# Tap sums and the turn of the filter gradient moved from the matmul stream to DMA and VectorE in the last phase

## The chip, the cores and the metric

The kernel runs on one core of a Trainium2 chip. The metric is the device time of one execution in microseconds (us), the median of several. Five engines work side by side, each through its own queue in order: TensorE (matmuls and weight loads), VectorE (in the profile DVE), ScalarE (ACT), GpSimd (POOL) and SyncE (SP), which here issues most of the DMA transfers. A DMA queue entry named SPq is the issue of a transfer by SyncE, not the movement of its bytes.

## The reference

With S = 2048 rows (time), D = 1024 channels and F = 3584:

```python
xn = layernorm(q)
k_shift = sum over t of shift(k, t) * shift_k[:, 3 - t]        # 4 taps, causal
kv = k_shift * v
y = causal_conv(kv, ssm_k) + kv * ssm_D                        # one filter of length S per channel
h = relu(xn @ W_gate) * (xn @ W_up)
out = q + xn * y + h @ W_down
```

It returns `out` and the gradients for q, k, v, shift_k, ssm_k, ssm_D, W_gate, W_up and W_down, given the gradient g of `out`, in bf16. Two of them matter here. With gks the gradient of k_shift, the gradient of shift_k is, for each channel c and tap i, the sum over time of gks[t, c] * k[t - i, c]: 4 numbers per channel. The gradient of ssm_k is gh[c, t], a row of 2048 per channel (channel-major), while the kernel's other tensors are time-major, [t, c].

## The kernel before

Two bodies of work share the core. `LnMlp` does the layer norm and the gated MLP with its gradients, nearly all large matmuls (128x128 weights, 512 columns), in phases: `hidden`, `grad_down`, `grad_in`, `out_phase`, `grad_x`. `ABranch` does the convolution by way of Fourier transforms, themselves small matmuls, for eight groups of 128 channels. Its steps are generators (`slots`, `wide_slots`): each `yield p, d` names a piece of TensorE work p and a piece of VectorE work d. The loop at the end of the kernel function interleaves the branch with the MLP's phases: every piece of MLP work takes its nanoseconds from a budget `left`, and while the budget is at or below zero the branch takes a step and gives back the price of its slot (`SLOT` 1900, or `DENSE` 1900 with TensorE work and 1250 without). The budget starts at `A_START`, so the branch starts that much later than the MLP. While the branch runs, each engine's instructions keep the order in which they are written. The branch ends before `grad_in` does; then `open_right` starts to load W_down for `out_phase`.

What the change touches, per group: `inv_b` is the last step of an inverse transform; it writes a tile time-major, with 64x32 weights and 512 columns (16 matmuls). `inv_b_chan` is the same step for the filter gradient, but with data as weights, 128x128 with 64 columns (32 matmuls), so that the result is channel-major (`ghn`), and `store_gh` writes it to `out_gh` in rows of 2 KB; it also copies element 0 of each row, the gradient of ssm_D, into `gD_all`. `tap_sums` multiplies, for each of 16 row blocks and each of 4 quarters of the channels, gks (128x32) with four shifted views of k (128 columns): 64 matmuls, of which only the diagonals are wanted. `tap_diagonals` takes them out on VectorE with an identity mask and a reduction into `gs_all`. At the end `small_outputs` turns the collected sums with six transposes on TensorE and stores them. `store_time` writes a time-major tile of 2048x128 to memory in two transfers with runs of 256 bytes.

`grad_x`, the last phase, goes over 16 tiles of 128 rows. For each it loads two tall tiles transposed by DMA (`ggT`, `guT`: 128 x 3584, turned, 28 blocks of 128x128; pool `hT` with three buffers), three row tiles (gt, gy, xn), runs 2 x 56 matmuls into two PSUM banks of four (`ps_x`), and VectorE evicts each with a sum and goes on to the layer norm's gradient:

```python
V.tensor_tensor_reduce(out=gx[:, oc], in0=ps, in1=gy[:, oc], scale=1.0, scalar=0.0, op0=ALU.add,
                       op1=ALU.add, accum_out=m[:, ob:ob + 1])
```

SyncE issues all of these transfers in one queue. In it stand, tile after tile, ggT of the next tile, gt, the two stores of the tile before, gy, xn, then guT.

Of the kernel before, what the change touches and what calls it, by code (L numbers as in the profile page):

```python
# [11 lines left out]
BF16 = mybir.dt.bfloat16  # L12
F32 = mybir.dt.float32
I32 = mybir.dt.int32
ALU = mybir.AluOpType
ACT = mybir.ActivationFunctionType
AX = mybir.AxisListType
P = 128
# [3 lines left out]
class Pri:  # L22
# [4 lines left out]
    def __init__(self, tc):  # L27
        self.tc = tc
        self.n = 0
        self.strict = False  # L30
# [15 lines left out]
NB1 = 32  # L46


class ABranch:
# [5 lines left out]
    def __init__(self, tc, pri, S, D, k, v, g, shift_k, ssm_k, ssm_D, xn_d, y_d, sk_d, out_gk, out_gv, out_gsk,  # L55
                 out_gh, out_gsD):
        assert S == 2048 and D % P == 0
        self.tc, self.nc, self.pri = tc, tc.nc, pri
        self.S, self.D, self.NG = S, D, D // P
        self.k, self.v, self.g, self.shift_k, self.ssm_k, self.ssm_D = k, v, g, shift_k, ssm_k, ssm_D  # L60
        self.xn_d, self.y_d, self.sk_d = xn_d, y_d, sk_d
        self.out_gk, self.out_gv, self.out_gsk, self.out_gh, self.out_gsD = out_gk, out_gv, out_gsk, out_gh, out_gsD
        self.pools, self.pin, self.dense, self.queue = [], False, False, []
        self.cap, self.turns = 2, 0
# [83 lines left out]
    def tables(self):  # L148
        nc, con, big, pri = self.nc, self.con, self.big, self.pri
        pri.late()  # L150
        V, hold = nc.vector, self.tc.keep_in_program_order
# [5 lines left out]
        self.gs_all = con.tile([P, self.NG, 4], F32, name="gs_all")  # L157
        self.gD_all = con.tile([64, 2, self.NG], BF16, name="gD_all")
# [77 lines left out]
        self.ident32 = con.tile([P, 1, 32], BF16, name="ident32")  # L236
        self.NX = con.tile([1, 3, P], BF16, name="NX")
        V.memset(self.NX[:], 0.0)
        for b in range(0, P, 32):
            V.tensor_copy(out=self.ident32[b:b + 32, 0, :], in_=self.identA[b:b + 32, b:b + 32])  # L240
# [81 lines left out]
    def load_taps(self, st):  # L322
        skb = st["skb"] = self.sm.tile([P, 4, 1, P], BF16, name="skb")
        self.load(skb[:].rearrange("p i o c -> p (i o c)"),
                  self.sk_d[4 * st["gi"]:4 * st["gi"] + 4, :].rearrange("i c -> (i c)").partition_broadcast(P))
# [174 lines left out]
    def inv_b_chan(self, st, half):  # L500
        dst, Cf = self.ttile("ghn"), self.flp[:, half]
        st["ghn"] = dst
        dv = dst[:, 0:16, :].rearrange("p r c -> p (r c)").rearrange("p (n1 n2) -> p n1 n2", n2=NB1)
        for n0 in range(0, NB1, 16):
            ps, at = self.banks("h n c", n=8)
            for n in range(16):
                self.mm(at(n // 8)[:, n % 8, :], Cf[:, n0 + n, :], self.RB[:].rearrange("p h n -> p (h n)"))
            self.evict(ps, "p h n c -> p c (h n)", lambda s: dv[:, :, n0 + 8 * s.start:n0 + 8 * s.stop])
        yield

    def store_gh(self, st):
        ghf = st["ghn"][:, 0:16, :].rearrange("p r c -> p (r c)")
        ghv = ghf.rearrange("p (h t) -> p h t", h=2)
        self.vcopy(self.gD_all[:, :, st["gi"]:st["gi"] + 1], ghv[0:64, :, 0:1])
        for b in range(2):
            self.store(self.out_gh[st["cg"], 1024 * b:1024 * b + 1024].rearrange("(h c) t -> c h t", h=2),
                       ghv[64 * b:64 * b + 64])
# [7 lines left out]

    def tap_sums(self, st):

        gks, kp = st["gks"], st["kp"]
        pd = self.banks("h x")[1](0)[:, 0:P].rearrange("p (i c) -> p i c", i=4)
        for r in range(16):  # L530
            for b in range(0, P, 32):
                self.mm(pd[b:b + 32], gks[:, r, b:b + 32], kp[:, r:r + 4, b:b + 32], start=(r == 0), stop=(r == 15))
        st["pd"] = pd

    def tap_diagonals(self, st):
        dg = self.tmp.tile([P, 4, 32], F32, name="dg", tag="tmp")
        self.tt(dg[:], st["pd"], self.ident32[:].to_broadcast([P, 4, 32]), ALU.mult)
        self.pri.late()
        self.pri.pin(self.nc.vector.tensor_reduce(out=self.gs_all[:, st["gi"], :], in_=dg[:], axis=AX.X, op=ALU.add))
# [33 lines left out]
    def steps(self):  # L573

        sk_t = self.shift_rows()
        self.pin = True
        yield 10000
        self.load(self.sk_d, sk_t[:])  # L580
        yield 25000
        self.sts = [dict(gi=gi, cg=slice(gi * P, (gi + 1) * P)) for gi in range(self.NG)]
        st = self.sts[0]
        self.load_filter(st)
        self.issue()
        yield 3400
        self.load_k(st)
        self.load_taps(st)
        yield 3400
        self.load_g(st)  # L590
        yield 3400
        self.load_v(st)
        yield 6800
        self.load_xn(st)
        self.pin = False
        self.pri.strict = True
        self.open_arena()
        self.begin(st)
        for st in self.sts:
            for p, d in (self.wide_slots if self.dense else self.slots)(st, st["gi"]):  # L600
                *more, last = self.parts(p)
                for fs in more:
                    self.all_of(fs)
                    yield self.DENSE[0]
                self.all_of(last)
                self.run(d)
                if self.queue and not self.hold():
                    self.issue()
                yield self.DENSE[p is None] if self.dense else self.SLOT
        self.small_outputs()  # L610
# [61 lines left out]
    def slots(self, st, gi):  # L672
# [57 lines left out]
        self.store_time(self.out_gv, st["cg"], gv)  # L730
        yield None, q
        yield None, self.both(lambda: self.halo(st), q)
        yield lambda: self.tap_sums(st), None
# [7 lines left out]
        yield None, lambda: self.tap_diagonals(st)  # L741
# [42 lines left out]
        yield self.inv_b_chan(st, 1), tk  # L784
        yield None, tk
        yield None, tk
        if last:
            yield None, lambda: self.store_gh(st)
            return
        self.need(self.load_v, nx)  # L790
        yield None, lambda: self.start_kvt(nx)
        f1k = self.fwd1(self.Bk, nx["kvt"])
        yield None, lambda: self.store_gh(st)
# [11 lines left out]
    def wide_slots(self, st, gi):  # L805
# [61 lines left out]
        self.store_time(self.out_gv, st["cg"], gv)  # L867
        yield None, q
        yield None, self.both(lambda: self.halo(st), q)
        yield lambda: self.tap_sums(st), None  # L870
# [7 lines left out]
        yield None, lambda: self.tap_diagonals(st)  # L878
# [43 lines left out]
        yield self.inv_b_chan(st, 1), tk  # L922
        yield None, tk
        yield None, None
        if last:
            yield None, lambda: self.store_gh(st)
            return
        self.need(self.load_v, nx)
        yield None, lambda: self.start_kvt(nx)
        f1k = self.fwd1(self.Bk, nx["kvt"])  # L930
        yield None, lambda: self.store_gh(st)
# [11 lines left out]
    def small_outputs(self):  # L943
        nc, NG = self.nc, self.NG
        tp = nc.tensor.transpose
        sk = self.sm.tile([P, NG, 4], BF16, name="sk_o", bufs=1)
        self.vcopy(sk[:], self.gs_all[:])
        ps = self.ps.tile([P, 1024], BF16, name="ps8", tag="aps")
        for i in range(4):
            self.pri.now()  # L950
            self.pri.pin(tp(ps[0:NG, i * P:(i + 1) * P], sk[:, :, 3 - i], self.identA[:]))
        for h in range(2):
            self.pri.now()
            self.pri.pin(tp(ps[0:NG, 4 * P + 64 * h:4 * P + 64 * h + 64], self.gD_all[:, h, :], self.identA[0:64, 0:64]))
        so = self.tmp.tile([NG, 5, P], BF16, name="so", tag="tmp")
        self.vcopy(so[:, 0:4, :].rearrange("g i c -> g (i c)").rearrange("g (c i) -> g i c", i=4),
                   ps[0:NG, 0:4 * P].rearrange("g (i c) -> g i c", i=4))
        self.vcopy(so[:, 4, :], ps[0:NG, 4 * P:5 * P])
        self.store(self.out_gsk.rearrange("(g c) i -> g (c i)", c=P), so[:, 0:4, :].rearrange("g i c -> g (i c)"))
        self.store(self.out_gsD.rearrange("(g c) -> g c", c=P), so[:, 4, :])  # L960
A_START = 60_000


class LnMlp:
# [742 lines left out]
    def grad_x(self, x, g, xn_d, y_d, h_d, ug_d, Wd, out0, out1):  # L1707
        nc, tc, D, V = self.nc, self.tc, self.D, self.nc.vector
        p_ev = tc.alloc_tile_pool(name="x_ev", bufs=2, side="right")
        p_sm = tc.alloc_tile_pool(name="x_sm", bufs=2, side="right")  # L1710
        for st in range(self.ST):
# [12 lines left out]
            if st == 1:  # L1724
                self.rest_load(x, xn_d, y_d, Wd)
            gx = p_ev.tile([P, D], F32, name="gx")
# [34 lines left out]
        self.p_rest.release()  # L1761
        p_sm.release()
# [8 lines left out]
def kernel(  # L1771
# [33 lines left out]

    sk_d = dram.tile([D // P * 4, P], BF16, name="sk_d")
# [3 lines left out]
    a = ABranch(tc, pri, S, D, A_k[0], A_v[0], g, A_shift_k, A_ssm_k, A_ssm_D, xn_d, y_d, sk_d[:], out_2[0], out_3[0],  # L1810
                out_4, out_5, out_6)
# [38 lines left out]
    b.grad_x(x, g, xn_d, y_d, h_d, ug_d, B_W_down, out_0[0], out_1[0])  # L1850
# [30 lines left out]
```

## Time and profile before

| | |
|---|---|
| time, median of 3 | 1876.04 us (1875.87 to 1876.24) |
| span of the profiled execution | 1874.5 us |
| TensorE busy | 1852.7 us, 99% |
| VectorE busy | 1050.2 us, 56% |
| ScalarE busy | 613.1 us, 33% |
| moved by DMA | 323.72 MB, mean 173 GB/s |
| the branch's matmuls | from 124.9 to 1244 us |
| `out_phase` begins | 1290.8 us |
| `grad_x` begins | 1478 us |

Busy time of an engine is the union of its instructions' spans. Matmuls overlap in the array, so TensorE's busy share says that it is occupied, not that it runs at its peak. A line of matmul groups gives weights, columns, count, busy time and mean duration of one; a window gives for each engine the busy time in that stretch, then the granted clock of TensorE, the mean busy share of the 16 DMA engines and the rate. That share can come out over 1, since records of packets overlap.

### The profile page before, as it was taken

The page shows a single profiled execution, that of the slowest core. Times are in us where ns is not written, and L with a number is a line of the kernel's source. Part 1 is how long each engine was busy: PE and PEld are TensorE (multiplying, and loading weights), DVE is VectorE, ACT ScalarE, POOL GpSimd, SP SyncE. Part 2 cuts the span into 40 slices and gives each one's busy share as a digit, 9 for nine tenths or more (in the row PEclk, how much of TensorE's full clock was granted, in tenths as well). Part 3 has the DMA queues.
Part 4 walks back from the last instruction along what each step waited for, and adds up shares of the span by engine and source line. Part 5 has one row for each costly group of instructions (what it writes and reads, how often), then busy time and mean ns, then how long its engine had stood idle before and what let it go on. Part 6 is the DMA issues. An engine that isn't in the chain of part 4 may idle for free.

```text
span 1874.5 us, 32572 instructions
## 1 busy us (share of the span) xinstructions
PE 1852.7 (99%) x13478; PEld 852.5 (45%) x13707; DVE 1050.2 (56%) x1537; ACT 613.1 (33%) x904; POOL 14.8 (1%) x37
## 2 busy tenths in 40 slices
PE   9999999999999999999999999999999999999999
PEld 4444444444444444444444444444444544444444
DVE  6656888699698677685585876710222222222222
ACT  5745444534445445444535454320000000000000
POOL 1000000000000000000000000000000000000000
PEclk9999999999999999999999999999999999999999
DMA  9897499868568747377465353479999945555553
GB/s 254 257 246 169 134 204 222 193 166 200 150 163 209 246 100 192 104 185 216 136 148 153 97 165 98 136 172 278 259 226 249 249 115 123 124 123 124 124 124 73
DMA packets 695509, 323.72 MB, mean 173 GB/s; under 512 B 524864, under 2 KB 664896, under 8 KB 695360
## 3 DMA queue, kind: packets, MB, share of 16 engines
q1 hardware_dynamic: 684864, 300.78, 65.1%
q10 hardware_dynamic: 9216, 16.65, 2.9%
q0 software_dynamic: 1280, 4.20, 0.6%
q8 instruction: 107, 1.75, 0.4%
q14 instruction: 42, 0.34, 0.1%
HBM read 143.79 MB, written 95.44 MB: 128 GB/s over the span
## 4 chain that ended last, share of the span: by engine, by line
PE 97%; issue 1%; DMA 1%; DVE 0%; SPq 0%; ACT 0%; POOL 0%; ACTq 0%; POOLq 0%
PE ps_x L1739 21%; PE ps_w L1503 20%; PE ps_u L1171 10%; PE ps_h L1171 10%; PE ps_o L1670 10%; PE ps_g L1171 10%; PE ps_d L1503 9%; PE ps L89 4%; PE ps_d L1518 1%; PE ps_c L89 1%; PE ps_w L1518 1%; PE ps_r L1700 0%; PE ps_warm L1226 0%; DMA wu<-in_B_W_up_dram 0%; SPq L1189 0%
## 5 line engine op out<-in xcount | busy, mean ns | idle before, releaser
L1503 PE MATMUL ps_w<-ugs,xn_nat 128*128 128x512 bf16 x1672 | 377.1, 380 | 4.5 <-issue 2.4
L1171 PEld LDWEIGHTS <-xnT 128*128 128x128 bf16 x1792 | 170.8, 98 | 208.9 <-issue 8.2
L93 ACT CAST arena<-ps 128x1024 bf16<-128x1024 f32 x240 | 234.3, 1021 | 72.2 <-PE ps L89 62.9
L1503 PEld LDWEIGHTS <-xn_nat 128*128 128x128 bf16 x1728 | 164.4, 98 | 201.3 <-issue 9.8
L344 DVE STREAM_TRANSPOSE arena<-arena 128x1024 f32<-128x1024 f32 x96 | 180.4, 1933 | 129.1 <-ACT arena L93 115.6
L1171 PE MATMUL ps_u<-wu,xnT 128*128 128x512 bf16 x875 | 205.3, 380 | 1.4 <-issue 0.3
L1171 PE MATMUL ps_g<-wg,xnT 128*128 128x512 bf16 x867 | 203.1, 380 | 2.4 <-issue 0.6
L1171 PE MATMUL ps_h<-wdT,goT 128*128 128x512 bf16 x862 | 202.8, 380 | 2.6 <-issue 0.8
L1757 ACT ACTIVATE w<-xn,m 128x512 f32<-128x512 bf16 x32 | 24.3, 806 | 553.0 <-issue 317.2
L1739 PE MATMUL ps_x<-wgT,ggT 128*128 128x512 bf16 x879 | 197.6, 379 | 0.9
L1739 PE MATMUL ps_x<-wuT,guT 128*128 128x512 bf16 x877 | 197.5, 379 | 1.0
L1670 PE MATMUL ps_o<-wd,hT 128*128 128x512 bf16 (+1 forms) x878 | 186.6, 373 | 0.9
L1503 PE MATMUL ps_d<-g_nat,hs 128*128 128x512 bf16 x740 | 168.8, 380 | 2.1 <-issue 0.8
L1739 PEld LDWEIGHTS <-guT 128*128 128x128 bf16 x896 | 87.7, 98 | 105.7
L1739 PEld LDWEIGHTS <-ggT 128*128 128x128 bf16 x896 | 87.7, 98 | 105.5
L1171 PEld LDWEIGHTS <-goT 128*128 128x128 bf16 x896 | 85.5, 98 | 105.4 <-issue 5.5
L1670 PEld LDWEIGHTS <-hT 128*128 128x128 bf16 x896 | 87.7, 98 | 100.0
L1506 ACT CAST wi<-ps_w 128x512 bf16<-128x512 f32 x108 | 63.8, 591 | 200.5 <-PE ps_w L1503 180.2
L1741 DVE CUSTOM_DVE_ANT_0 gx<-ps_x,gy 128x512 f32<-128x512 f32 x32 | 22.1, 692 | 185.3 <-PE ps_x L1739 175.4
L1413 ACT CAST gh<-ps_h 128x512 bf16<-128x512 f32 x112 | 65.5, 585 | 184.1 <-PE ps_h L1171 173.2
L1286 DVE SCALAR_TENSOR_TENSOR ru<-ru,ps_u 128x512 bf16<-128x512 bf16 x112 | 76.5, 684 | 81.9 <-PE ps_u L1171 44.4
L97 DVE TENSOR_TENSOR t<-arena 128x2048 bf16<-128x2048 bf16 x96 | 114.1, 1219 | 0.4
(165 smaller groups left out, 1341.6 us busy)
## 6 DMA issues: line engine op xcount, KB each, us to landing
ug_d<-ru SPq DMA_DIRECT2D x112, 256.0 KB
ugs<-ug_d SPq DMA_DIRECT2D x112, 256.0 KB
wg<-in_B_W_gate_dram SPq DMA_DIRECT2D x56, 256.0 KB
wu<-in_B_W_up_dram SPq DMA_DIRECT2D x56, 256.0 KB
h_d<-ht SPq DMA_DIRECT2D x112, 128.0 KB
hs<-h_d SPq DMA_DIRECT2D x56, 256.0 KB
out_dram<-wi SPq DMA_DIRECT2D x56, 256.0 KB
gt<-in_grad_out_dram SPq DMA_DIRECT2D x32, 256.0 KB
```

Source lines behind the costliest of these rows:

```text
L89: self.pri.pin(self.nc.tensor.matmul(out, lhsT=lhsT, rhs=rhs, start=start, stop=stop))
L93: self.pri.pin(self.nc.scalar.copy(out=out, in_=in_))
L97: self.pri.pin(self.nc.vector.tensor_tensor(out=out, in0=in0, in1=in1, op=op))
L344: self.pri.pin(self.nc.vector.transpose(out=df[:, c0:c0 + 32, :], in_=sf[:, c0:c0 + 32, :]))
L1171: self.pri.pin(self.nc.tensor.matmul(ps[:], lhsT=xT[:, kt * P:(kt + 1) * P], rhs=w(kt), start=(kt == 0), stop=(kt == self.DT - 1)), always ...
L1286: return self.pri.pin(nc.vector.scalar_tensor_tensor(out=ru[s][:, 1, :], in0=ru[s][:, 0, :], scalar=0.0, in1=ps[:], op0=ALU.is_gt, op1=ALU ...
L1413: self.pri.pin(nc.scalar.copy(out=gh[:], in_=ps[:]))
L1503: self.pri.pin(self.nc.tensor.matmul(ps[:], lhsT=lhsT(st), rhs=rhs(st), start=(st == 0), stop=(st == self.ST - 1)))
L1506: self.pri.pin(self.nc.scalar.copy(out=out, in_=ps[:]))
L1518: self.pri.pin(self.nc.tensor.matmul(ps[i][:], lhsT=lhsT(i, st), rhs=rhs(i, st), start=(st == 0), stop=(st == self.ST - 1)))
L1670: nc.tensor.matmul(ps, lhsT=hT[:, kt, :], rhs=self.wd[:, kt, oc], start=(kt == 0), stop=(kt == self.FT - 1))
L1739: nc.tensor.matmul(ps, lhsT=T[:, kt, :], rhs=W[:, kt, oc], start=(i == 0), stop=(i == n - 1))
```

## The change

The tap sums leave TensorE. gks is written to memory (`gks_d`) by the branch, and in `grad_x` three transposes by DMA per group of channels bring gks, k and gh as [channel, time] rows; VectorE multiplies and sums gks with the shifted k, eight instructions per group, in the row tiles 3 to 10. The filter gradient's last step becomes `inv_b`, time-major; it is written to `gh_d`, comes back turned (`ghT`) and goes from there to `out_gh`. The gradient of ssm_D is row 0 of gh, stored directly. `tap_sums`, `tap_diagonals`, `inv_b_chan` and `small_outputs` go, and their slots with them; `A_START` goes from 60,000 to 72,000 ns.

```diff
     def store_gh(self, st):
-        ghf = st["ghn"][:, 0:16, :].rearrange("p r c -> p (r c)")
-        ghv = ghf.rearrange("p (h t) -> p h t", h=2)
-        self.vcopy(self.gD_all[:, :, st["gi"]:st["gi"] + 1], ghv[0:64, :, 0:1])
-        for b in range(2):
-            self.store(self.out_gh[st["cg"], 1024 * b:1024 * b + 1024].rearrange("(h c) t -> c h t", h=2),
-                       ghv[64 * b:64 * b + 64])
+        self.store(self.out_gsD[st["cg"]].rearrange("(o c) -> o c", o=1), st["gh"][0:1, 0, :])
+        self.store_time(self.gh_d, st["cg"], st["gh"])
...
         self.store_time(self.out_gv, st["cg"], gv)
+        self.store_time(self.gks_d, st["cg"], gks)
         yield None, q
         yield None, self.both(lambda: self.halo(st), q)
-        yield lambda: self.tap_sums(st), None
...
-        yield None, lambda: self.tap_diagonals(st)
...
-        yield self.inv_b_chan(st, 1), tk
+        yield self.inv_b(st, "gh", 1), tk
...
         yield None, lambda: self.start_kvt(nx)
+        self.store_gh(st)
         f1k = self.fwd1(self.Bk, nx["kvt"])
-        yield None, lambda: self.store_gh(st)
+        yield None, None
...
-A_START = 60_000
+A_START = 72_000
...
+    TAPS_AT = 3
+
+    def open_taps(self):
+        self.p_tap = self.tc.alloc_tile_pool(name="x_tap", bufs=2, side="right")
+        self.p_gs = self.tc.alloc_tile_pool(name="x_gs", bufs=1, side="right")
+        self.gs = self.p_gs.tile([P, 2, self.DT, 4], F32, name="gs")
+
+    def load_taps(self, g, gks_d, gh_d, k):
+
+        cg = slice(g * P, (g + 1) * P)
+        self.rows = []
+        for name, src in (("gksT", gks_d), ("kT", k), ("ghT", gh_d)):
+            t = (self.p_gs if src is gh_d else self.p_tap).tile([P, self.S], BF16, name=name)
+            self.nc.sync.dma_start_transpose(out=t[:], in_=src[:, cg])
+            self.rows.append(t)
+
+    def taps(self, g, out_gh, pool):
+        gksT, kT, ghT = self.rows
+        self.nc.sync.dma_start(out=out_gh[g * P:(g + 1) * P, :], in_=ghT[:])
+        h = self.S // 2
+        for i in range(4):
+            for b in range(2):
+                n = h - i * (1 - b)
+                junk = pool.tile([P, self.D], BF16, name="pr")
+                self.nc.vector.tensor_tensor_reduce(
+                    out=junk[:, 0:n], in0=gksT[:, max(b * h, i):b * h + h], in1=kT[:, max(b * h - i, 0):b * h + h - i],
+                    scale=1.0, scalar=0.0, op0=ALU.mult, op1=ALU.add, accum_out=self.gs[:, b, g, i:i + 1])
...
             if st == 1:
                 self.rest_load(x, xn_d, y_d, Wd)
+            group = st - self.TAPS_AT
+            if 0 <= group < self.DT:
+                self.taps(group, out_gh, p_ev)
+            if group == self.DT:
+                self.store_taps(out_gsk)
+            if 0 <= group + 1 < self.DT:
+                self.load_taps(group + 1, gks_d, gh_d, k)
```

## The prediction

> **What bounds the kernel now.** I read the totals and the chain on the page first, then the matmul groups with shapes kept apart, then the chain of waits around single bursts, and for the last phase the windows by stage and the timeline of SyncE.
>
> ```profile
> span 1874.5 us, 32572 instructions
> ...
> PE 1852.7 (99%) x13478; PEld 852.5 (45%) x13707; DVE 1050.2 (56%) x1537; ACT 613.1 (33%) x904; POOL 14.8 (1%) x37
> ...
> PE 97%; issue 1%; DMA 1%; DVE 0%; SPq 0%; ACT 0%; POOL 0%; ACTq 0%; POOLq 0%
> ```
>
> TensorE is busy from end to end, its granted clock is 1.00 in every window, and nothing else holds more than 1% of the chain. Where no stall is made, a microsecond of matmul taken away is a microsecond off the span; VectorE's 56% is not a bound. Matmuls overlap, so a group's busy time is not its price. That is read in the chain, which lays the pieces end to end:
>
> ```profile
> 303.59 0.93 PE ps L89 x32
> ...
> 703.48 1.01 PE ps L89 x64
> ...
> 1194.33 0.16 issue
> ...
> 1229.96 0.34 PE ps L89 x8
> 1230.30 0.21 PE ps_c L89 x8
> ...
> 1243.64 0.32 PE ps L951 x4
> 1243.96 0.15 PE ps L954 x2
> ```
>
> Columns: start, duration, what. x64 is one `tap_sums`, x32 one `inv_b_chan`, the two x8 one `inv_b` (of gkv; the same shape as the new one of gh), the last two the transposes of `small_outputs`. "issue" pieces come about every 49 matmuls, 0.05 to 0.16 us each. The groups with shapes:
>
> ```profile
> L89 PE MATMUL ps<-kp,gks 128*32 128x128 bf16 x448 | 7.5, 220 | 0.0
> L89 PE MATMUL ps<-RB,arena 128*128 128x64 bf16 x208 | 7.4, 193 | 0.0
> ```
>
> The last phase is where the new work goes:
>
> ```profile
> 1502.20:1526.40 24.20, 24.09 (x112) 10.97 (x112) 6.84 (x16) 1.52 (x2) 0.00 (x0) 1.00 0.50 119
> ```
>
> A row tile takes 24.2 us, 24.09 of it TensorE, 6.84 VectorE, DMA share 0.50 at 119 GB/s. Inside such a tile, SyncE:
>
> ```profile
> 1502.45 3.50 SPq L1636 DMA_TRANSPOSE ggT<-ug_d  x1
> ...
> 1508.15 0.41 SPq L1722 DMA_DIRECT2D xn<-xn_d  x1
> 1520.59 3.52 SPq L1636 DMA_TRANSPOSE guT<-ug_d  x1
> 1526.63 3.76 SPq L1636 DMA_TRANSPOSE ggT<-ug_d  x1
> ```
>
> SyncE issues nothing between 1508.6 and 1520.6: it stands before guT, whose buffer (three hT buffers) comes free when the running tile is done with its ggT. And the phase before shows what the transfers can do:
>
> ```profile
> 1310.00:1322.10 12.10, 12.05 (x57) 5.47 (x56) 2.67 (x4) 0.00 (x0) 0.00 (x0) 1.00 1.21 241
> 1322.10:1334.20 12.10, 12.05 (x57) 5.46 (x56) 2.77 (x4) 0.00 (x0) 0.00 (x0) 1.00 1.15 275
> ```
>
> Half transposes, half copies, 241 to 275 GB/s, and TensorE still 12.05 of 12.10 us busy.
>
> **What the Trainium skill says.** "TensorEngine Tiling (Array Packing)", Key Properties: tiles of the array work in parallel, and a change of tiling mode drains TensorE. The trace agrees with the first (64 matmuls of 219 ns each in 1.01 us) and fits the second (at the 216 ns between two N = 512 matmuls, N = 128 streams in 54, and 64 x 54 / 4 = 0.86 us is less than the 1.01). "DMA: Bandwidth & Descriptors", Latency and other measured facts: a transpose by DMA ran at 261 GB/s. The trace agrees: 243 and 210 GB/s in the two slices of 2 us (1522 to 1526) that hold one guT. "VectorE: DVE Perf Modes", the perf-mode tier table: tensor_tensor in bf16 from SBUF runs two elements a cycle, in fp32 one. Agreed below; tensor_tensor_reduce isn't listed there.
>
> **The change, part by part.**
> 1. `tap_sums` goes: 8 bursts x 1.01 = 8.1 us of chain.
> 2. `inv_b` replaces `inv_b_chan` for the filter gradient: 0.93 against 0.34 + 0.21 = 0.55, 8 x 0.38 = 3.0 us.
> 3. `small_outputs` goes: 0.32 + 0.15 = 0.5 us.
> 4. About 1,290 PE instructions fewer (512 matmuls and their weight loads, 128 and theirs, 6 transposes). At one "issue" piece per 49 matmuls and loads, 13 pieces of 0.05 to 0.16: 0.7 to 2 us; I take 0.8.
> Sum 12.4 us. All four lie on the chain.
> 5. VectorE loses `tap_diagonals` (286 + 291 ns x 8 = 4.6 us) and the gD copies; ScalarE's evictions keep their size (ghn 1024, gkv 1026 ns). Worth nothing: TensorE hides them.
> 6. Two stores of gks more per group; those of gh become 256 B rows. They add 0.5 MB and some 1.4 us of SyncE issue per group (a pair of gv stores takes 1.45 us at 242.9), beside a group of 75 to 120 us. gks is older than gv, stored just before, so the queue meets no new wait. In the first 300 us the DMA share is above 0.9 and SyncE issues without a pause around 240, so a later weight load may slip by 1 to 2 us; weights are loaded a block ahead. Cost 0 to 3 us, taken as 0.
> 7. Two slots fewer per group (1900 + 1250 or 2 x 1900) against a start 12 us later (`A_START`): the branch ends some 14 us of matmul time earlier, so the wd loads, which now start at 1264.5 and end before 1290.8, have more room. Nothing.
> 8. Last phase, DMA: per row tile, in eight tiles, three transposes of 2048x128. One ggT is 28 blocks of 128x128 and takes about 4.1 us of transfer (the 2 us slices from 1522 have shares 1.11 and 0.93), so 48 blocks take 7.0 us; the out_gh store of 0.5 MB at 250 GB/s takes 2. 4.98 MB per 24.2 us is 206 GB/s, below the 241 that the phase before sustains. SyncE: 3.5 us per 28 blocks gives 6 us for 48, plus 0.5; the gap of 12 us holds it. ghT has one buffer, so its transpose waits for the out_gh store just issued, some 4 us (gy landed 4.2 us after its issue); queued behind it is guT. Even at 1524 rather than 1520.6 it lands by 1530, and its first matmul is at 1526.4 + 28 x 0.216 = 1532.5.
> 9. Last phase, VectorE: eight tensor_tensor_reduce of 1024 bf16 per tile. Not in the trace; the neighbours are:
>
> ```profile
> L1743 DVE CUSTOM_DVE_ANT_0 pr<-gx,xn 128x512 bf16<-128x512 f32 x32 | 22.2, 692 | 1.1
> L97 DVE TENSOR_TENSOR t<-t,u 128x1024 bf16<-128x1024 bf16 x96 | 66.4, 692 | 3.3
> L97 DVE TENSOR_TENSOR t<-arena 128x2048 bf16<-128x2048 bf16 x96 | 114.1, 1219 | 0.4
> ```
>
> The same instruction takes 692 ns for 512 in f32; a bf16 product two at a time takes 692 for 1024 and 1219 for 2048, so 512 steps cost 530 ns. One element a step: 1222 + some 40 of accumulator read, 10.1 us for eight; two a step: 5.8. I take 10.1: VectorE 17 of 24.2 us. Behind them in its queue waits the eviction of ps_x; four banks of 12.1 us each give TensorE over 30 us before it lacks one. Hidden.
>
> So 1876.04 - 12.4 = 1863.6.
>
> **The rivals.**
> (a) A small stall comes back. For: SyncE works in order, so a tap transpose waiting for its buffer (or an o1 store behind late VectorE sums) holds back guT, and the first 300 us have little DMA to spare. Against: 6 us between guT's landing and its use, and 9.5 us per tile without DMA (1512 to 1521.5). About 0.5 to 1 us in each of eight tiles, or 1 to 3 us early: 1866 to 1872.
> (b) The last phase becomes DMA-bound: the column slices of 256 B rows 2 KB apart may transpose at half the rate of ggT. Then 12.1 + 14 + 2 = 28.1 us of transfer per 24.2, 3.9 x 8 = 31 us, less some 7 of slack: 1863.6 + 24 = 1888, slower. Against: ggT too is read in 256 B pieces a row apart (the page counts 524,864 packets under 512 B), and goT, xnT come from 2 KB rows without a visible wait.
> (c) More gain: the drains around mixed tilings and the larger "issue" pieces give 2 us more: 1861.
>
> **How the numbers follow.** Forecast 0.70 (1862 to 1866); (a) 0.16, of which 0.05 within 0.2%; (b) with other slower ends 0.09; (c) 0.05. Time 1863.6. Low 1861.0 takes in most of (c), high 1871.0 most of (a); (b) is left out. Faster (below 1872.3) 0.86, same 0.05, slower 0.09.
>
> **What would show it.** Right: no group over kp and gks, no 128x64 group over RB; PE busy 11 to 12 us lower; row tiles in the last phase still 24.2 us; DMA share there about 0.85 to 0.9, VectorE 13 to 17 us per tile; no SyncE wait that delays guT beyond its first use. Wrong: PE idle before ps_x for DMA or VectorE, tiles over 24.5 us between about 1520 and 1740, or a slower group around 240 to 320.

## The result, and the profile after

| | median us | runs | ratio to before, 95% interval |
|---|---|---|---|
| before | 1876.14 | 1875.87 to 1876.33 | |
| after | 1891.12 | 1887.89 to 1895.99 | 1.0082 [1.006, 1.0104] |

The kernel became 15 us slower; 12.4 us faster was forecast, and the time lies far over the range. The page after, with totals and chain as shown of before:

```profile
span 1890.0 us, 31459 instructions
...
PE 1849.7 (98%) x12837; PEld 839.7 (44%) x13061; DVE 1118.8 (59%) x1635; ACT 613.9 (32%) x905; POOL 14.8 (1%) x37
...
PE 81%; DMA 3%; DVE 2%; SPq 2%; issue 1%; DVEq 0%
```

The recorded matmuls fell from 13,478 to 12,837. Both traces miss nearly 2% of them; by the weight loads, 13,707 and 13,061, there are 646 fewer, the 512, 128 and 6 of the forecast. And yet TensorE was busy for only 3 us less, where 11 to 12 were forecast. Its share of the chain fell from 97 to 81%: now DMA, VectorE and SyncE's issues stand in it. The waits of TensorE, in all and longest (total us, times, longest us), say for what:

```profile
PE ps_x L1727 <- DMA guT<-ug_d: 7.7, 4, 2.9
PE ps_g L1117 <- DMA wg<-in_B_W_gate_dram: 3.8, 3, 2.7
PE ps_u L1117 <- DMA wu<-in_B_W_up_dram: 3.5, 5, 1.4
```

Two places, then: guT in the last phase, and the weights of `hidden`, the first phase. The start of the first matmul of three phases in each trace divides the span:

| first matmul, us | before | after | paced | both |
|---|---|---|---|---|
| `grad_down` (ps_d) | 642.2 | 655.9 | 658.1 | 641.4 |
| `out_phase` (ps_o) | 1290.7 | 1296.8 | 1299.0 | 1281.7 |
| `grad_x` (ps_x) | 1478.1 | 1484.2 | 1486.4 | 1469.1 |
| the rest of q (ps_r) | 1864.9 | 1880.8 | 1873.2 | 1855.9 |
| from ps_x to ps_r | 386.8 | 396.6 | 386.8 | 386.8 |

(`paced` and `both` are experiments below.) After, `grad_x` takes 9.8 us longer, and 13.7 us are lost before `grad_down`. Between `grad_down` and `out_phase` the kernel is 7.6 us quicker (640.9 against 648.5), so there the removed matmuls do pay.

**The last phase.** SyncE's timeline (start, duration, issue):

```profile
1526.87 2.00 SPq L1666 DMA_TRANSPOSE ghT<-gh_d  x1
1531.10 0.34 SPq L1671 DMA_DIRECT2D out_dram<-ghT  x1
1533.75 1.24 SPq L1666 DMA_TRANSPOSE ghT<-gh_d  x1
1535.08 4.95 SPq L1582 DMA_TRANSPOSE guT<-ug_d  x1
...
1548.41 3.66 SPq L1666 DMA_TRANSPOSE ghT<-gh_d  x1
1554.13 0.34 SPq L1671 DMA_DIRECT2D out_dram<-ghT  x1
1556.77 1.85 SPq L1666 DMA_TRANSPOSE ghT<-gh_d  x1
1560.70 0.34 SPq L1671 DMA_DIRECT2D out_dram<-ghT  x1
1561.13 4.29 SPq L1582 DMA_TRANSPOSE guT<-ug_d  x1
```

There is not one ghT per row tile but two or three, with the stores that empty it, and guT stands behind them. In the source each ghT belongs to its group's row tile; in the queue all eight have gone by 1592.7, within some four tiles. The chain of waits through these lines shows what each costs:

```profile
1548.41 5.71 DMA ghT<-gh_d
1554.13 2.62 DMA out_dram<-ghT
1556.77 3.91 DMA ghT<-gh_d
1560.70 0.34 SPq L1671
1561.13 6.65 DMA guT<-ug_d
1567.82 6.23 PE ps_x L1727 x28
```

Transpose lands, store leaves, next transpose lands, and each of them holds the queue: 12.7 us before guT is issued. TensorE's timeline, with the idle time ahead of a burst and what ended it in brackets:

```profile
1542.09 6.22 PE L1727 MATMUL ps_x<-wuT,guT 128*128 128x512 bf16 x28 [2.83 <-DMA guT<-ug_d]
...
1567.82 6.22 PE L1727 MATMUL ps_x<-wuT,guT 128*128 128x512 bf16 x28 [1.39 <-DMA guT<-ug_d]
```

Four tiles wait: 0.57 + 2.83 + 1.39 + 2.95 = 7.7 us. Part of the other 2.1 of the 9.8 is in what follows a wait. In windows (start and end, length, then busy time of PE, PEld, DVE, ACT, POOL, then clock, DMA share, GB/s):

```profile
1592.00:1595.10 3.10, 0.17 (x1) 0.00 (x0) 2.78 (x10) 0.75 (x2) 0.00 (x0) 0.98 1.14 245
1595.10:1598.10 3.00, 2.98 (x8) 1.06 (x9) 1.38 (x2) 0.76 (x2) 0.00 (x0) 0.50 1.24 268
1542.00:1545.00 3.00, 2.91 (x14) 1.38 (x15) 0.00 (x0) 0.00 (x0) 0.00 (x0) 1.00 1.12 242
```

After the wait of 2.95 us the clock is 0.50 for about 3 us: 8 matmuls where the same time after the wait of 2.83 us holds 14. At 0.216 us each, the 6 missing make that wait 1.3 us dearer than it shows. "TensorE: Matmul & The Clock Gate", Part 1: The HAM clock gate, in the Trainium skill says that an idle stretch of about 3.4 us brings the array down to half rate. The traces agree on the half rate, but not on a length from which it sets in. Of the waits for guT in two variants described below, one of 2.23 us (a60) was followed by slow matmuls, 28 in 7.84 us instead of 6.22:

```profile
1587.40 7.84 PE L1727 MATMUL ps_x<-wuT,guT 128*128 128x512 bf16 x28 [2.23 <-DMA guT<-ug_d]
```

and one of 3.08 us (ghact60) was not:

```profile
1528.42 6.22 PE L1727 MATMUL ps_x<-wuT,guT 128*128 128x512 bf16 x28 [3.08 <-DMA guT<-ug_d]
```

So the length of one wait alone does not decide it; what else does, no run here shows.

A tile late in the phase, when ghT is through, is as forecast in length:

```profile
1633.70:1657.90 24.20, 24.04 (x111) 10.96 (x113) 16.75 (x34) 1.52 (x2) 0.00 (x0) 1.00 0.76 173
```

**The first phase.** The same windows over the first 650 us, of before:

```profile
0.00:650.00 650.00, 641.72 (x4985) 292.49 (x5071) 499.27 (x782) 307.81 (x455) 13.15 (x33) 1.00 0.79 200
320.00:340.00 20.00, 19.84 (x184) 8.75 (x185) 11.25 (x14) 10.08 (x15) 0.00 (x0) 1.00 1.03 229
```

and of after:

```profile
0.00:650.00 650.00, 631.17 (x4656) 282.12 (x4739) 488.31 (x762) 304.83 (x450) 13.57 (x34) 0.99 0.81 197
320.00:340.00 20.00, 16.43 (x75) 6.24 (x75) 10.32 (x14) 6.15 (x9) 0.41 (x1) 0.83 0.97 250
```

TensorE is busy for 10.5 us less, and part of what is busy runs at a lower clock (0.83 in the 20 us shown). In those 20 us the DMA share is about 1 in both traces (over the 650 us it is 0.79 and 0.81), so there a load that comes late can hardly catch up, and its place in the queue counts. The worst stall of after, in TensorE's timeline:

```profile
328.99 1.87 PE L1117 MATMUL ps_g<-wg,xnT 128*128 128x512 bf16 x4 [2.68 <-DMA wg<-in_B_W_gate_dram]
```

Four matmuls in 1.87 us: half rate again.

### The profile page after: what moved, and what is told of

It is laid out like the page before. It is cut to its first block, busy times and chain, and to the rows that moved or that the text cites. A ratio compares the mean times of both kernels' runs of the same rounds, so it can differ in the third digit from the quotient of the medians.

```text
span 1890.0 us, 31459 instructions
## 1 busy us (share of the span) xinstructions
PE 1849.7 (98%) x12837; PEld 839.7 (44%) x13061; DVE 1118.8 (59%) x1635; ACT 613.9 (32%) x905; POOL 14.8 (1%) x37
## 4 chain that ended last, share of the span: by engine, by line
PE 81%; DMA 3%; DVE 2%; SPq 2%; issue 1%; DVEq 0%
PE ps_w L1449 20%; PE ps_x L1727 17%; PE ps_o L1616 10%; PE ps_d L1449 9%; PE ps_u L1117 7%; PE ps_g L1117 6%; PE ps_h L1117 6%; PE ps L89 4%; PE ps_d L1464 1%; SPq L1582 1%; DMA ghT<-gh_d 1%; PE ps_c L89 1%; PE ps_w L1464 1%; DMA guT<-ug_d 1%; DVE arena L339 1%
## 5 line engine op out<-in xcount | busy, mean ns | idle before, releaser
L1117 PEld LDWEIGHTS <-xnT 128*128 128x128 bf16 x1792 | 171.6, 98 | 225.9 <-issue 27.5
L93 ACT CAST arena<-ps 128x1024 bf16<-128x1024 f32 x243 | 238.2, 1021 | 87.4 <-PE ps L89 77.1
L1117 PE MATMUL ps_u<-wu,xnT 128*128 128x512 bf16 x876 | 209.4, 384 | 5.5 <-DMA wu<-in_B_W_up_dram 3.5
L1608 DVE TENSOR_TENSOR ya<-ya,xe 128x1024 bf16<-128x1024 bf16 x16 | 11.1, 693 | 201.7 <-DMA xe<-xn_d 201.7
L97 DVE TENSOR_TENSOR t<-arena 128x2048 bf16<-128x2048 bf16 x96 | 113.8, 1219 | 0.5
```

The source lines that it names most:

```text
L93: self.pri.pin(self.nc.scalar.copy(out=out, in_=in_))
L97: self.pri.pin(self.nc.vector.tensor_tensor(out=out, in0=in0, in1=in1, op=op))
L1117: self.pri.pin(self.nc.tensor.matmul(ps[:], lhsT=xT[:, kt * P:(kt + 1) * P], rhs=w(kt), start=(kt == 0), stop=(kt == self.DT - 1)), always ...
```

## The experiments

The theory was: two separate losses. In `grad_x` the order of SyncE's queue; in `hidden` weight loads that come late, because of the later start (`A_START`), of the new stores of gks, or of both. Rivals: the last phase lacks DMA bandwidth; the branch's faster pace (two slots fewer per group) is to blame. The kernel before ran beside each set: median 1877.28 with the first four, 1876.64 with the next four, 1876.99 with the last two.

**1. paced: the tap transfers tied to their row tile.** The kernel after, with the tap transposes and the store of ghT issued only after that tile's xn load:

```diff
-            nc.sync.dma_start(out=xn[:], in_=xn_d[rows, :])
+            self.xn_load = nc.sync.dma_start(out=xn[:], in_=xn_d[rows, :])
...
-            self.nc.sync.dma_start_transpose(out=t[:], in_=src[:, cg])
+            with self.tc.issue_after(self.xn_load.ins):
+                self.nc.sync.dma_start_transpose(out=t[:], in_=src[:, cg])
...
-        self.nc.sync.dma_start(out=out_gh[g * P:(g + 1) * P, :], in_=ghT[:])
+        with self.tc.issue_after(self.xn_load.ins):
+            self.nc.sync.dma_start(out=out_gh[g * P:(g + 1) * P, :], in_=ghT[:])
```

> The changed kernel, with the tap transposes and the out_gh store held in SyncE's queue behind the xn load of their own row tile, so that the ghT transposes can't run several tiles ahead. Theory Q (SyncE stands in front of guT, waiting for ghT to land and for out_gh to free its one buffer): no matmul of ps_x waits for guT any more, grad_x falls from 396.6 us to 387 (as before the change), the time from 1891 to about 1881. Rival B (the transfers themselves are the bound while taps are loaded): guT stays late, grad_x stays above 392, the time above 1886.

Measured: 1884.86 us (1880.52 to 1886.59), ratio 1.0038 [1.0023, 1.0053]. `grad_x` is back at 386.8 us and TensorE never waits for guT. The bytes are the same, so it was the order and not the bandwidth. The first phase is as slow as after, or 2 us slower (the table above), and the time is 4 us over the 1881 expected.

**2. a60: the old start.** The kernel after with one line undone:

```diff
-A_START = 72_000
+A_START = 60_000
```

> The changed kernel with A_START back at 60,000. Theory S (the later start of the branch puts its loads beside the MLP's weight loads): the waits for wg and wu in the first 650 us go, ps_d starts near 642 us less what the removed matmuls save, the time falls from 1891 to 1872 to 1876. Rival W (the added stores of gks and gh delay the weight loads): the waits stay, time 1888 to 1893.

Measured: 1880.1 us (1875.39 to 1884.09), ratio 1.0015 [1.0008, 1.0021]. The waits for wg and wu are gone (0.4 us are left), and `grad_down` begins at 643.1. But the time is 4 us over the range expected: `grad_x` took 403.2 us in its trace against after's 396.6, with other waits for guT. The loss in the last phase stays and hides part of the gain. (The trace is of the slowest of the 20 runs, 4 us over their median, so 403 is not the usual figure.)

**3. b72: the late start alone**, in the kernel before:

```diff
-A_START = 60_000
+A_START = 72_000
```

> The kernel before with A_START at 72,000 and nothing else. Theory S: 1885 to 1895 with waits for wg and wu in the first 650 us. Rival W: 1876, within 2 us, since the stores aren't there.

Measured: 1882.52 us (1880.21 to 1885.99), ratio 1.0031 [1.0021, 1.0042]. A start 12 us later costs by itself, 5 to 6 us, a little less than the theory expected. SyncE's timeline of b72 where the first stall of TensorE lies (1.9 us for wu in three parts between 141 and 145):

```profile
129.11 2.68 SPq L105 DMA_DIRECT2D gt<-in_grad_out_dram  x2
131.84 2.41 SPq L105 DMA_DIRECT2D sD<-in_A_ssm_D_dram  x1
...
135.65 1.37 SPq L105 DMA_DIRECT2D vt<-in_A_v_dram  x2
...
138.72 2.06 SPq L1164 DMA_DIRECT2D wu<-in_B_W_up_dram  x4
```

and of before:

```profile
119.57 1.43 SPq L105 DMA_DIRECT2D gt<-in_grad_out_dram  x2
121.05 1.83 SPq L105 DMA_DIRECT2D sD<-in_A_ssm_D_dram  x1
...
132.91 1.97 SPq L1164 DMA_DIRECT2D wu<-in_B_W_up_dram  x4
```

With the later start the branch's first loads (gt, sD, vt) stand right in front of a weight load that is due; it is issued 5.8 us later, while the wg load before it goes at 126.6 in both.

**4. bgks: the stores alone.** The kernel before, with two stores of gks per group that nobody reads:

```diff
         self.store_time(self.out_gv, st["cg"], gv)
+        self.store_time(self.gks_d, st["cg"], gks)
```

> The kernel before with the two gks stores per group added and nothing else (the copy isn't read). Theory S: 1876 to 1878. Rival W: 1884 to 1892 with waits for wg and wu around 280 to 430 us.

Measured: 1878.35 us (1877.24 to 1881.71), ratio 1.0008 [0.9999, 1.0016]. At the old start the stores cost about 1 us; the interval goes from nothing to 3.

**5. both: experiments 1 and 2 together.**

> The changed kernel with both edits: the tap transfers held behind xn of their own row tile, and A_START at 60,000. Theory Q + S (two separate losses, one in grad_x by SyncE's queue, one in hidden by the branch's start): grad_x takes 387 us and starts near 1470, no matmul waits for guT, wg or wu, and the time is 1866 to 1869. If all of the forecast's 12.4 us is there, it is 1864. Rival (the losses share a cause, and mending one gives back to the other): 1874 or more.

Measured: 1865.96 us (1865.14 to 1866.89), ratio 0.9942 [0.9929, 0.9954]: faster than before and after. Its page:

```profile
PE 1842.2 (99%) x12836; PEld 838.4 (45%) x13061; DVE 1120.6 (60%) x1635; ACT 613.1 (33%) x904; POOL 14.8 (1%) x37
...
PE 96%; DMA 2%; issue 1%; DVE 0%; SPq 0%; ACT 0%; ACTq 0%
```

TensorE is busy for 10.5 us less than before. The two edits give 25 us together, but 6 and 11 alone: the losses lie in two places, yet a change of the start also changes the order in the last phase (experiment 2). SyncE's timeline in a row tile:

```profile
1524.24 0.38 SPq L1705 DMA_DIRECT2D xn<-xn_d  x1
1524.67 0.42 SPq L1673 DMA_DIRECT2D out_dram<-ghT  x1
1525.15 4.28 SPq L1667 DMA_TRANSPOSE gksT<-gks_d  x1
1529.47 2.11 SPq L1667 DMA_TRANSPOSE kT<-in_A_k_dram  x1
1531.67 1.94 SPq L1667 DMA_TRANSPOSE ghT<-gh_d  x1
1535.80 3.52 SPq L1582 DMA_TRANSPOSE guT<-ug_d  x1
```

One of each per tile, and the store of ghT is 7 us ahead of the transpose that needs its buffer. One of its tiles, in a window:

```profile
1518.20:1542.40 24.20, 24.09 (x112) 11.00 (x113) 16.46 (x33) 1.52 (x2) 0.00 (x0) 1.00 0.88 207
```

This is the tile that the prediction described: 24.2 us, 207 GB/s, VectorE 16.5 us, no idle time of TensorE.

**6. ghact60: another queue for the store.** The kernel a60 with the store of ghT issued by ScalarE:

```diff
-        self.nc.sync.dma_start(out=out_gh[g * P:(g + 1) * P, :], in_=ghT[:])
+        self.nc.scalar.dma_start(out=out_gh[g * P:(g + 1) * P, :], in_=ghT[:])
```

> The changed kernel with A_START at 60,000 and the out_gh store issued by ScalarE's queue; the ghT transposes may still run several tiles ahead. Theory Q: only the wait for ghT's landing leaves SyncE; the wait for the one ghT buffer stays in front of guT, so that of the 16 us that grad_x lost with A_START at 60,000 (403 against 387) between a third and all stays: grad_x 390 to 403. Rival (it is the store's own wait alone that holds guT): grad_x 387.

Measured: 1879.94 us (1876.43 to 1883.55), ratio 1.0016 [1.0008, 1.0024]; `grad_x` 399.1 us. The ratio is that of a60 (1.0015), so it doesn't help. (That `grad_x` is 4 us shorter than in a60's trace says little, since that trace is of a run 6 us slower than this one.) In SyncE's timeline two ghT stand in front of guT, now waiting in the queue for a store that another engine issues:

```profile
1512.32 8.71 SPq L1666 DMA_TRANSPOSE ghT<-gh_d  x2
1521.13 4.35 SPq L1582 DMA_TRANSPOSE guT<-ug_d  x1
```

So it isn't the store's place in SyncE's queue that holds guT, but a transpose that waits for its only buffer there. The edit also has a side effect: ScalarE's own work now stands behind the store, and once begins only after 36 us, when ghT has landed. A second buffer for ghT would test the same from the other side; it wasn't tried.

**7. nogks72: the stores taken away at the late start.** The kernel paced without the two stores of gks per group; gksT is read from k, so the gradient of shift_k is left out, while every transfer and sum of the last phase stays:

```diff
-        self.store_time(self.gks_d, st["cg"], gks)
...
-        for name, src in (("gksT", gks_d), ("kT", k), ("ghT", gh_d)):
+        for name, src in (("gksT", k), ("kT", k), ("ghT", gh_d)):
```

> The changed kernel with the tap transfers held as in the first experiment and A_START at 72,000, without the gks stores; gksT is read from k, so the shift_k gradient is left out. Against the held kernel at 1885. If the added stores share the blame in hidden: the waits for wg and wu around 280 and 430 us go and the time falls by 3 to 8 us. If the start alone is to blame: the same waits, 1883 to 1886.

Measured: 1876.69 us (1875.36 to 1879.31), ratio 1.0001 [0.9992, 1.0009], 8.2 us under paced (6.9 by the ratios). Of the waits for wg and wu, those around 280 are gone and 0.35 us is left around 430; those at 143 and 327 stay, and in all TensorE still waits 3.7 us for wg and 1.6 for wu.

**8. slots72: the branch's old pace at the late start.** The kernel paced with two empty slots per group put back:

```diff
+        yield None, None
+        yield None, None
```

> The changed kernel with the tap transfers held, A_START at 72,000, and two empty slots per group in place of the two that went with the tap sums. If the branch's faster pace shares the blame in hidden (its loads and evictions fall on other MLP blocks): fewer waits for wg and wu after 250 us, as in the kernel before with the later start (1882.5), less the removed matmuls: 1870 to 1876. If not: 1883 to 1887.

Measured: 1884.17 us (1881.4 to 1885.4), ratio 1.0037 [1.0023, 1.0051]: nothing against paced. The waits fall on other loads (5.5 us for wu, 1.8 for wg, 2.0 for xn_nat in `grad_down`), but the pace is not to blame for the time.

**9. nogks60: the fourth corner.** The kernel nogks72 with `A_START` 60,000:

> The paced order of the last phase, the start at 60,000, and the stores of gks left out (gksT read from k, so the gradient of shift_k is left out). It is the fourth corner of stores by start: with stores and 60,000 the time was 1865.96, with stores and 72,000 1884.86, without stores and 72,000 1876.69. If the stores and the later start do harm only together (theory: both crowd the same queue in the first 430 us), this run is within 1 us of 1866, since nothing was left to gain there. If each costs by itself, it is 8 us better than with stores, 1858. If the stores hold even at 60,000 the bit that is missing between the 10.7 us measured and the 12.4 forecast, it is 1864.

Measured: 1865.62 us (1865.35 to 1865.85), ratio 0.9941 [0.9926, 0.9956]. With the paced order in all four:

| us | start at 60,000 | start at 72,000 |
|---|---|---|
| stores of gks | 1865.96 | 1884.86 |
| without | 1865.62 | 1876.69 |

At the old start the stores show no cost (ratios 0.9942 and 0.9941): this run is as the theory had it, within 1 us of 1866. At the late start they cost 7 to 8 us (by ratios and by times), and the late start costs 11 us even without them, so it is the first cause and the stores add to it. In the kernel before, the same later start cost only 5 to 6 us (experiment 3). What makes it dearer in the changed kernel stays open: the pace was ruled out with the stores in place (experiment 8), but the stores of gh, which the change turned from rows of 2 KB into rows of 256 bytes, are in every variant of the changed kernel and were not varied.

**10. both66: the start half way.** The kernel both with `A_START` 66,000:

> The paced order, with stores, the start half way at 66,000. If the loss grows evenly with the later start (1865.96 at 60,000, 1884.86 at 72,000), it is 1875. If it is a matter of which loads of the branch stand in front of which weight load (theory), it is a step: near 1866 or near 1884, with waits of PE for wg and wu in the second case and hardly any in the first.

Measured: 1877.4 us (1874.33 to 1880.48), ratio 1.0 [0.9991, 1.0008]. It lies between, near the even growth; the step that the theory asked for isn't there. TensorE waits 5.9 us for wu and hardly for wg, and 2.3 us for xn_nat in `grad_down`: other loads are late than at 72,000.

## Why the prediction failed

**Steps 1 to 3, the matmuls taken away: right. Step 4: nothing there.** Together they were put at 12.4 us, 11.6 of it steps 1 to 3. With both losses gone, the time is 10.7 us under before's beside it (experiment 5; the ratio's interval goes from 8.6 to 13.3 us) and 11.4 under it in experiment 9; TensorE is busy for 10.5 us less. The 0.8 us of step 4 came from "issue" pieces in the chain. These are matmuls missing from the record, not time: the trace of before lists 13,478 matmuls beside 13,707 weight loads. That of b72 has the same matmuls and lists them all, and in its chain the pieces are gone:

```profile
PE 1868.7 (99%) x13707; PEld 852.6 (45%) x13707; DVE 1049.7 (56%) x1537; ACT 613.9 (33%) x906; POOL 14.8 (1%) x37
...
PE 90%; DMA 0%; SPq 0%; DVE 0%; issue 0%
```

TensorE's busy time can thus be compared only between traces that miss equally many, as before, after and both do.

**Step 5 and step 9, VectorE: right.** The sums were taken at one element a step, 1222 ns. The groups of experiment 5 (columns as before: count, busy us, mean ns, idle):

```profile
L1679 DVE CUSTOM_DVE_ANT_0 pr<-gksT,kT 128x1024 bf16<-128x1024 bf16 x40 | 48.9, 1223 | 0.8
...
L1679 DVE DVE_READ_ACCUMULATOR2_ANT gs<- 128x1 f32 x64 | 5.3, 83 | 0.0
```

VectorE has 16.5 us per tile against 17 forecast, and TensorE never waits for it in `grad_x`. The accumulator's read was put at 40 ns and takes 83, as the same reads do in the trace of before.

**Step 6, the stores, and step 7, the start: failed.** Step 6 said "weights are loaded a block ahead. Cost 0 to 3 us, taken as 0". Step 7 looked at where the branch ends and wrote "Nothing". Each was priced alone and at one end. Experiment 9's table has what took their place: 0 for the stores at the old start, 11 us for the late start without them, 18 to 19 us for both. The prediction had seen that SyncE issues without a pause around 240 and that DMA is nearly full in part of this phase ("above 0.9" in all the first 300 us is a misreading: in windows of 50 us before's share is 1.07, 0.84, 0.96, 0.62, 0.67 and 0.91). It did not ask what a start 12 us later moves in that queue: the branch's first loads land in front of weight loads that are due (seen at 138.72 in experiment 3), and the longest stall, of 2.68 us, is followed by matmuls at half rate. Which transfer is in front of each of the later stalls, and why 66,000 delays other loads, was read in the timelines only and not taken apart by runs.

**Step 8, the transfers of the last phase: the rate right, the order wrong.** The 206 GB/s were met (207). The step that failed is "its transpose waits for the out_gh store just issued, some 4 us", once per tile, with a guT that "lands by 1530". That wait came, of 2.6 to 3.3 us, but with it one that the sum does not have: the store waited for the transpose before it to land, 3.9 to 5.7 us. And they came in a row. The prediction took the order of the source for the order of the queue. ghT and its store depend on nothing in the row tile, only on each other, and in this phase the written order is no longer kept, so the scheduler let them run ahead, and two or three such waits stood in front of one guT. The chance was seen in rival (a), a tap transpose that waits for its buffer and holds back guT, and sized at 0.5 to 1 us in each of eight tiles; it was 0.6 to 3 us in four, and half rate after the longest. Undoing it gave 6 to 8 us at the late start (after to paced, by times and by ratios) and 14 at the old one (a60 to both).

**The rivals.** (a) named the mechanism of one loss, and its 2 to 8 us stand against the 27.5 between forecast and time. (b) gave 1888, near the time measured by luck, for its cause is refuted: the same transposes run at 207 GB/s, without a wait of TensorE, once their order is right. A time that fits is no evidence for the cause.

The signs listed in advance did tell: TensorE idle before ps_x for DMA, longer tiles from 1515 to 1600, and a slow stretch around 280. Those around 143, 329 and 429 lie outside the 240 to 320 that it named.

## What to carry to other kernels

A transfer that waits for its buffer in an in-order queue costs what stands behind it, so ask of every new one how many of its kind can be in front of the transfer that is due. If nothing ties a load and store chain on one buffer to the loop it is written in, tie it. And where DMA is full and TensorE just keeps up, a change of start time or a small store is not free because its price, worked out alone, comes to nothing: try each, and both together.

## What the runs showed of the hardware

- Waits of TensorE of 2.23 us (a60) and 2.95 us (after) were followed by about 3 us at a clock of 0.50; waits of 2.83 us (after) and 3.08 us (ghact60) were not. Where the half rate comes, it cost 1.3 to 1.6 us on top of the wait; the length of the wait alone does not tell whether it comes.
- Kernels whose loads come late also spread more from run to run: before's 35 runs beside the first experiments lie within 3.6 us, a60's 20 within 8.7, and the 5 of both within 1.8.
- tensor_tensor_reduce on bf16 took 1223 ns for 1024 elements (both), the time of 2048 in a plain bf16 product (1219, before).
